# Attention feeding a top-1 mixture of experts on one core: the start, the row stores and the key tails of the attention stage written in another order and form

## The chip, the core and the metric

The kernel runs on one core of a Trainium2 chip. Its engines run side by side, each with an instruction stream of its own: TensorE (PE, with PEld for weight loads), VectorE (DVE), ScalarE (ACT), GpSimd (POOL), and SyncE (SP), which here only issues DMAs. The metric is the device time of one execution in microseconds (us), the median of several runs. Lower is better.

## The reference

Attention with capped scores over q, k, v of shape (4, 12, 448, 64), then eight experts of which each row takes the best one:

```python
scores = np.matmul(q, k.transpose(0, 1, 3, 2)) / np.sqrt(64)
scores = cap * np.tanh(scores / cap)
attn = softmax(scores)                       # over the keys
x = (attn @ v).transpose(0, 2, 1, 3).reshape(1792, 768)
logits = x @ w_gate                          # 8 experts
prob = softmax(logits);  eom = sigmoid(x @ w_output_gate)
for e in range(8):
    mask = logits.argmax(1) == e
    h = relu(x[mask] @ w1[e])                # 768 -> 1024
    out[mask] = prob[mask, e] * eom[mask, e] * (h @ w2[e])
```

The sum over the keys doesn't depend on their order. Products are made in three terms from planes hi and lo of each operand (hi is the operand rounded to fp32r, lo the rest).

## The kernel before

Attention runs over 24 units u (NU = 24); a unit is one batch and two heads, j = 0 and 1, which fill 128 partitions (64 each). Batch 2 is units 12 to 17, batch 3 units 18 to 23. For each unit the loop at L969 does, in this order of the program: three score blocks of 128 keys for both heads and one block for the "tail", the last 64 keys of both heads side by side (`qk`, matmuls L386 and L391, tanh on ACT into the tile `pt`, L393); the DMAs that are due (`load_ahead`); the K and Q planes of units to come (`turn_next`, DVE: a 32x32 block transpose L288, casts to hi L278, subtracts to lo L284); `exp` over the whole `pt` (L396, ACT); probabilities times V of the unit before (`pv`, L404); the evacuation of that result; the partial sums of the exponentials (`presum`, L413, L414, L418). Between these stand named slots ("f", "g", "h", "q", "e"), in which the work of the batch before (gate logits, row transposes, routing) is hung by a table `at`.

What sets the order around the change:

- `pt` has two buffers. The tanh of unit u+2 writes the buffer of unit u, and so comes after `presum(u)` and `pv(u)`. POOL does `presum` for units 0 to 19, DVE for units 20 to 23.
- Score blocks, row transposes (`trow`, L586) and gate results share three PSUM buffers in turn (`scores`). PE can't start the next block before the reader of the third last has finished.
- A tail's K planes are block diagonal: head 0's 64 keys on partitions 0 to 63, head 1's on 64 to 127, zeros elsewhere. Five pairs of K planes (PB = 5) are zeroed once at the start (L190, L191, twenty memsets), and each unit's tails are cast and subtracted as two separate 64x64 pieces.
- K and Q of units 3 and up come as raw tiles, for two units at a time in four DMAs (`load_pair`, L124). The numbers in `TURN` (L59) say how many of the plane preparations are made before and after the exponential of each unit; where it has no entry, (2, 0).
- Rows of the attention output go from `xr` tiles (L591, DVE) to the DRAM table `xs` by two DMAs each (L598). There are three `xr` buffers in turn. The six rows tasks of batch 2 are `rws[0]` to `rws[5]` (units 19 to 21), so `rws[3]` writes the buffer that `rws[0]` filled and must come after its store. The stores are kept in a list and issued on SP by `store_rows`, at the end of each unit and where the table says so.
- `load_v` (L110, L142) loads V of two units in six DMAs on SP: main part of u, tails of both, main part of u+1. The tails overwrite those of the units four before, and so come after `pv` of the later of these.
- `early()` is a routine of small steps on DVE (`nx`) which works out the first experts' row tables (tile `meta`, L646 to L656). `fd` fetches those tables by DMA (L849), `lds` loads expert weights (L826).
- At the start, POOL clears the tables in DRAM from the tile `tabi` (L220, L223), before its first `presum`; DVE makes the scale of the tanh (`icap`, L173, L174) and the constant `epsc`.

After the last unit the experts run (php and py, L1084) up to the end.

Of the kernel before, what the change touches and what calls it, by code (L numbers as in the profile page):

```python
# [22 lines left out]
def tile_kernel(ctx: ExitStack, tc, q, k, v, cap, w_gate, w_ogate, w1, w2, out):  # L23
    nc = tc.nc
# [10 lines left out]
    NE = 5  # L35
# [14 lines left out]
    for i, kind in enumerate((2, 4)):  # L50
# [9 lines left out]
            14: (2, 1), 15: (2, 1), 16: (1, 0), 17: (1, 0), 19: (1, 0), 20: (1, 0), 21: (0, 0)}  # L60
# [47 lines left out]
    def load_natural(dst, src, n, m, engs):  # L108
        for j in range(2):
            engs[j].dma_start(out=dst[:, 0:n, j], in_=src[j, 0:n * m].rearrange("(c p) d -> p c d", c=n))  # L110

    def load_nat(u, engs):
        (k0, q0), k_, q_ = nat[u], heads(k, u), heads(q, u)
        load_natural(k0, k_, NK, 128, engs)
        engs[1].dma_start(out=k0[0:64, NK], in_=k_[:, SK:S].rearrange("j p d -> p j d"))
        load_natural(q0, q_, NCH, CP, engs)

    def load_pair(src, u, tiles, to):
        t = raw1[tiles[u // 2 % 3]][:, 0:2 * S].rearrange("p (h r a) -> p h r a", h=2, a=32)
        lo = u % 2  # L120
        for c in range(4):
            x = c % 2
            h = c // 2 * NP + u % NP
            nc.sync.dma_start(  # L124
                out=t[32 * c:32 * c + 32, lo:].rearrange("p h r a -> p (h r) a"),
                in_=src[u // NP, h:h + 2 - lo, :, 32 * x:32 * x + 32].rearrange("h (r b) a -> b (h r) a", b=32))
        for i in range(lo, 2):
            to[u + i - lo] = t[:, i]

    def load_k(u):  # L130
        load_pair(k, u, (0, 1, 4), ldk)
# [64 lines left out]
    nc.vector.memset(ohc, 0.0)  # L198
    for p in range(NP):
        nc.vector.memset(ohc[:, p, p:p + 1], 1.0)  # L200

    wg = rtp.tile([128, NP, 2, 16], F32, name="wg")
    nc.vector.memset(wg, 0.0)
# [13 lines left out]
    tabi = rtp.tile([128, NTAB // 128, 2], F32, name="tabi")  # L217

# [38 lines left out]
    for g in range(4):  # L257
        for z, x in enumerate((2 * NT + g // 2, 4 * NT + g, 6 * NT + g, 6 * NT + 4 + g)):
            nc.vector.memset(part[32 * g:32 * g + 32, z:z + 1], float(x))
# [26 lines left out]
    def turned(src, n):  # L286
        ps = tbank([128, n], "tk")
        nc.vector.transpose(out=ps, in_=src.rearrange("p r a -> p (r a)"))  # L288
        return ps
# [21 lines left out]
    def first_planes(pk, pq):  # L311
        k_, (main, *tails) = k_parts(0, pk)
        q_, (q0,) = q_parts(0, pq)
        copy(True, main[0], main[2])
        copy(True, q0[0], q0[2])
        for x, z, y in (main, q0):
            minus(z, y, x)
        for x, z, y in tails:
            copy(False, x, y)
            minus(z, y, x)  # L320
        return k_ + q_

    def t_k(u):
        pl[u] = planes_of(k_parts(u, turned(ldk.pop(u), S)))
# [131 lines left out]
    def end_of_batch(b):  # L456
# [512 lines left out]
    for u in range(NU):  # L969
        if u % 2:  # L970
            load_v(u + 1)
        for s in range(NK):
            qk(u, s)
        if u == 0:
            pl[1] = planes_of(k_parts(1, nat_k(1)))
        if u > 0:
            load_ahead()
        qk(u, NK)
        if u == 0:
            pl[1] += planes_of(q_parts(1, nat_q(1)))  # L980
            nc.vector.memset(tabi, 0.0)
            load_wg()
            clear_tabs()
        if u == 1:
            pl[2] = planes_of(k_parts(2, nat_k(2)))
            pl[2] += planes_of(q_parts(2, nat_q(2)))
# [7 lines left out]
        if u > NU - 4:  # L994
            presum(u - 1, 0)
            presum(u - 1, 1)
# [10 lines left out]
        if u < NU - 4:  # L1007
            presum(u, 0)
        slot(u, "e")
# [350 lines left out]
```

## Time and profile before

| what | value |
|---|---|
| median of 3 runs | 515.81 us (515.36 to 515.87) |
| the profiled execution, its own time | 514.19 us |
| its span in the trace | 512.6 us |
| PE busy | 488.6 us, 95% |
| DVE busy | 381.3 us, 74% |
| ACT busy | 371.7 us, 73% |
| POOL busy | 288.8 us, 56% |

The profiled execution is 1.6 us below the median of the runs, and its time is 1.6 us more than the span. PE is the busiest engine, but the share is a mean over stages. Attention takes about the first 200 us, the experts the rest. The windows, the timelines of single engines and the ends of their idle time tell which engine the others wait for in each stage.

### The profile page before, as it was taken

The page shows a single profiled execution, that of the slowest core. Times are in us where ns is not written, and L with a number is a line of the kernel's source. Part 1 is how long each engine was busy: PE and PEld are TensorE (multiplying, and loading weights), DVE is VectorE, ACT ScalarE, POOL GpSimd, SP SyncE. Part 2 cuts the span into 40 slices and gives each one's busy share as a digit, 9 for nine tenths or more (in the row PEclk, how much of TensorE's full clock was granted, in tenths as well). Part 3 has the DMA queues.
Part 4 walks back from the last instruction along what each step waited for, and adds up shares of the span by engine and source line. Part 5 has one row for each costly group of instructions (what it writes and reads, how often), then busy time and mean ns, then how long its engine had stood idle before and what let it go on. Part 6 is the DMA issues. An engine that isn't in the chain of part 4 may idle for free. (4 is left out here: it accounts for less than half of the span.)

```text
span 512.6 us, 10021 instructions
## 1 busy us (share of the span) xinstructions
PE 488.6 (95%) x3069; PEld 341.1 (67%) x3069; DVE 381.3 (74%) x746; ACT 371.7 (73%) x433; POOL 288.8 (56%) x310
## 2 busy tenths in 40 slices
PE   7899999999999988999999999999999999999994
PEld 6444455444545543678989979988788867686691
DVE  7669999798686897988999878867676857555550
ACT  5888988889887868556589878858676867665551
POOL 4999998888988614962268861317265035352001
PEclk9999999999999989999999999999999999999998
DMA  6879868484532548884099336259759689991001
GB/s 144 168 134 162 142 108 144 91 146 83 87 70 49 86 61 287 316 271 130 2 350 407 115 104 245 62 207 368 272 191 394 263 308 362 336 359 67 1 33 49
DMA packets 152380, 91.92 MB, mean 179 GB/s; under 512 B 135027, under 2 KB 135163, under 8 KB 152321
## 3 DMA queue, kind: packets, MB, share of 16 engines
q1 hardware_dynamic: 142336, 58.24, 43.6%
q0 software_dynamic: 8832, 32.74, 17.3%
q8 instruction: 26, 0.43, 0.4%
q10 hardware_dynamic: 1152, 0.25, 0.2%
q14 instruction: 34, 0.27, 0.2%
HBM read 123.68 MB, written 12.04 MB: 265 GB/s over the span
## 5 line engine op out<-in xcount | busy, mean ns | idle before, releaser
L1063 DVE TENSOR_TENSOR wr<-raw,wr 128x768 fp32r<-128x768 f32 (+1 forms) x167 | 172.8, 1073 | 64.4 <-ACT wr L1062 63.5
L1062 ACT ACTIVATE wr<-raw 128x768 fp32r<-128x768 f32 (+1 forms) x167 | 150.6, 936 | 28.1 <-PE py L1084 12.4
L393 ACT ACTIVATE pt<-s,icap 128x896 f32<-128x896 f32 x96 | 80.1, 914 | 17.1 <-PE s L386 9.9
L404 PE MATMUL u<-pt,vv 128*64 128x448 f32 x384 | 79.1, 555 | 1.5 <-ACT pt L393 1.1
L1084 PE MATMUL py<-wr,hh 128*128 128x384 f32 x352 | 77.3, 340 | 0.0
L1084 PE MATMUL php<-wr,xh 128*128 128x512 f32 x264 | 74.8, 404 | 0.0
L1153 POOL DMA_INDIRECT out_dram<-yo,ti x13 | 21.7, 1668 | 90.8 <-ACT yo L1151 67.4
L396 ACT ACTIVATE pt<-pt,capc 128x3136 f32<-128x3136 f32 x24 | 69.9, 2912 | 0.6
L1084 PEld LDWEIGHTS py<-wr,hh 128*128 128x128 f32 x352 | 61.2, 188 | 4.0 <-issue 3.7
L1084 PEld LDWEIGHTS php<-wr,xh 128*128 128x128 f32 x264 | 47.4, 188 | 12.8 <-issue 2.5
L418 POOL TENSOR_TENSOR pb<-pb,pt 64x448 f32<-64x448 f32 x42 | 49.6, 1181 | 10.1 <-DVE pb L414 7.0
L404 PEld LDWEIGHTS u<-pt,vv 128*64 128x64 f32 x384 | 25.9, 139 | 42.6 <-issue 34.7
L413 POOL TENSOR_TENSOR pa<-pt 128x896 f32<-128x896 f32 x20 | 42.3, 2114 | 10.8 <-ACT pt L396 10.0
L1084 PE MATMUL py<-wr,hl 128*128 128x384 f32 x176 | 44.8, 335 | 0.0
L414 POOL TENSOR_TENSOR pb<-pa,pt 128x896 f32<-128x896 f32 x20 | 42.1, 2103 | 1.6
L1084 PE MATMUL php<-wr,xl 128*128 128x512 f32 x132 | 41.6, 396 | 0.9 <-DVE xl L878 0.9
L1084 PEld LDWEIGHTS py<-wr,hl 128*128 128x128 f32 x176 | 31.8, 188 | 0.0
L1200 POOL DMA_DIRECT2D rh<-in_moe_w_dram x42 | 23.2, 557 | 15.0 <-DVE wr L1063 8.9
L1084 PEld LDWEIGHTS php<-wr,xl 128*128 128x128 f32 x132 | 24.7, 187 | 7.3 <-DVE xl L878 1.3
L288 DVE STREAM_TRANSPOSE tk<-raw 128x448 f32<-128x448 f32 x42 | 27.5, 654 | 0.9
L1254 POOL DMA_INDIRECT out_dram<-yh,toh x6 | 6.1, 1011 | 35.5 <-issue 13.9
L591 DVE TENSOR_TENSOR xr<-trow,rec 112x512 f32<-112x512 f32 x24 | 16.1, 687 | 10.7 <-PE trow L586 9.7
(315 smaller groups left out, 812.2 us busy)
## 6 DMA issues: line engine op xcount, KB each, us to landing
raw<-in_moe_w_dram SPq DMA_DIRECT2D x78, 512.0 KB
raw<-in_moe_w_dram SPq DMA_DIRECT2D x104, 384.0 KB
rh<-in_moe_w_dram POOLq DMA_DIRECT2D x18, 512.0 KB, 7.2
rh<-in_moe_w_dram POOLq DMA_DIRECT2D x24, 384.0 KB, 8.6
raw<-in_q_dram SPq DMA_DIRECT2D x45, 112.0 KB
vv<-in_v_dram SPq DMA_DIRECT2D x48, 96.0 KB
raw<-in_k_dram SPq DMA_DIRECT2D x40, 112.0 KB
xs<-xr SPq DMA_DIRECT2D x36, 112.0 KB
```

What stands on the lines that cost most here:

```text
L288: nc.vector.transpose(out=ps, in_=src.rearrange("p r a -> p (r a)"))
L393: nc.scalar.activation(out=pt[u][:, 2 * s:2 * s + n], in_=ps, func=ACTF.Tanh, scale=icap)
L396: nc.scalar.activation(out=pt[u], in_=pt[u], func=ACTF.Exp, scale=capc)
L404: nc.tensor.matmul(ups[u][64 * j:64 * j + 64], lhsT=V[:, c, j, :], rhs=P[:, 2 * c + (j if c < NK else 0)], start=(c == 0), stop=(c == NK))
L413: eng.tensor_tensor(out=a, in0=P[:, 0:2], in1=P[:, 2:4], op=ALU.add)
L414: eng.tensor_tensor(out=s1[u], in0=a, in1=P[:, 4:6], op=ALU.add)
L418: eng.tensor_tensor(out=s1[u][h, j], in0=s1[u][h, j], in1=P[h, 2 * NK], op=ALU.add)
L1062: nc.scalar.activation(out=t[:, 0, 0:F], in_=raw, func=ACTF.Copy)
L1063: nc.vector.tensor_tensor(out=t[:, 1, 0:F], in0=raw, in1=t[:, 0, 0:F].bitcast(F32), op=ALU.subtract)
L1084: nc.tensor.matmul(ps[g][:, 0:n], lhsT=st[:, c], rhs=w[:, z, g * n:(g + 1) * n], start=(c == 0 and st is hi and z == 0), stop=(c == (KD, K ...
L1153: nc.gpsimd.indirect_dma_start(out=out, out_offset=bass.IndirectOffsetOnAxis(ap=ti, axis=0), in_=y, in_offset=None, bounds_check=NT - 1, o ...
L1200: nc.gpsimd.dma_start(out=d, in_=rows_of(src, e, w, c), **kw)
```

## The change

The diff has five parts.

1. Zeros and key order. The raw K tiles now hold 16 blocks of 32 columns for each unit: blocks 0 and 1 are head 0's first 64 keys (zeros for head 1), blocks 14 and 15 are head 1's last 64 keys (zeros for head 0). Head 0's tail is so its first 64 keys (T0 = 64) and head 1's its last 64; the V loads follow the same order. The zeros of the raw tiles are set once (six memsets). From unit 3 on a K preparation is two transposes (384 and 128 columns), one cast and one subtract of 128x512, with no separate tails. Only three pairs of K planes are still zeroed.
2. K loads. A pair of K tiles now comes in eight DMAs of half the size; Q is loaded as before.
3. Start. On DVE `icap` is made between the two first subtracts; `epsc`, the tails, `ohc` and `part` come later, and for units 1 and 2 the main part, Q and then the tails are made. POOL zeroes `wg` and `tabi` itself, ahead of all that it loads.
4. End of attention, SP: the last V load (units 22, 23) moves from the start of unit 21 into slot "q" of unit 20, ahead of `rws[1]` to `rws[3]` and of `store_rows`.
5. End of attention, DVE: `presum` of units 20 to 22 stands at the end of its own unit, not after the exponential of the next; the `nx` steps move behind the stores of unit 21; `TURN` prepares units 22 and 23 earlier or in other places.

```diff
-            14: (2, 1), 15: (2, 1), 16: (1, 0), 17: (1, 0), 19: (1, 0), 20: (1, 0), 21: (0, 0)}
+            14: (2, 1), 15: (2, 1), 16: (1, 0), 17: (1, 0), 20: (1, 0), 21: (0, 1), 22: (0, 0)}
...
+    def load_k(u):
+        t = kview[u // 2 % 3]
+        for i in range(u % 2, 2):
+            for c in range(4):
+                j, x = divmod(c, 2)
+                nc.sync.dma_start(
+                    out=t[32 * c:32 * c + 32, i, 2 * j:2 * j + 14],
+                    in_=blocks(k[u // NP, j * NP + u % NP + i - u % 2], x).rearrange("(r b) a -> b r a", b=32))
+            ldk[u + i - u % 2] = t[:, i]
...
-    for hl in kpl:
+    for hl in kpl[0:NN]:
...
+    for t in kview:
+        nc.vector.memset(t[0:64, :, 14:16], 0.0)
+        nc.vector.memset(t[64:128, :, 0:2], 0.0)
...
-    nc.vector.memset(wg, 0.0)
+    nc.gpsimd.memset(wg, 0.0)
...
+    nc.gpsimd.memset(tabi, 0.0)
...
+            nc.vector.transpose(out=ps[:, 0:SK], in_=src[:, 2:14].rearrange("p r a -> p (r a)"))
+            nc.vector.transpose(out=ps[:, SK:].rearrange("p (n k) -> p n k", n=2),
+                                in_=src.rearrange("p (n r) a -> p n (r a)", r=2)[:, 0::7])
...
+        if u >= NN:
+            return [hi, lo], [(hi, lo, ps)]
...
+            minus(main[1], main[2], main[0])
+            scales()
+        minus(q0[1], q0[2], q0[0])
...
-                  (1, "g"): [rws[0], rank_mm, place], (1, "h"): [place2, enter, scatter], (1, "q"): [rws[1], rws[2], rws[3], store_rows],
-                  (1, "e"): [nx] * 5,
-                  (2, "g"): [rws[4], rws[5]], (2, "h"): [nx, P(set_known, NE), store_rows],
-                  (2, "q"): [fd[0], fd[1], *lds[:2]],
+                  (1, "g"): [rws[0], rank_mm, place], (1, "h"): [place2, enter, scatter], (1, "q"): [P(load_v, NU - 2), rws[1], rws[2], rws[3], store_rows],
+                  (2, "g"): [rws[4], rws[5]], (2, "h"): [store_rows, *[nx] * 6, P(set_known, NE)],
+                  (2, "q"): [fd[0], *lds[:2], fd[1]],
...
-        if u % 2:
+        if u % 2 and u < NU - 3:
             load_v(u + 1)
...
-        if u > NU - 4:
-            presum(u - 1, 0)
-            presum(u - 1, 1)
...
-        if u < NU - 4:
+        if u < NU - 1:
             presum(u, 0)
+        if NU - 4 <= u < NU - 1:
+            presum(u, 1)
```

PE's and ACT's instructions keep their order; what moves is on DVE, POOL and SP. On DVE at the start, before (`tk` is unit 0's K turned by PE; the 64x64 rows are its tails):

```order
L284 TENSOR_TENSOR K0L<-tk_293,K0H 128x384
L284 TENSOR_TENSOR QL<-tq_298,QH 128x448
L278 CAST K0H<-tk_293 64x64
L284 TENSOR_TENSOR K0L<-tk_293,K0H 64x64
L278 CAST K0H<-tk_293 64x64
L284 TENSOR_TENSOR K0L<-tk_293,K0H 64x64
L173 RECIPROCAL icap<-capc 128x1
L174 TENSOR_SCALAR icap<-icap 128x1
L178 TENSOR_SCALAR epsc<-capc 128x1
L179 TENSOR_TENSOR epsc<-epsc,capc 128x1
```

and now:

```order
L302 TENSOR_TENSOR K0L<-tk_269,K0H 128x384
L186 RECIPROCAL icap<-capc 128x1
L187 TENSOR_SCALAR icap<-icap 128x1
L302 TENSOR_TENSOR QL<-tq_274,QH 128x448
L296 CAST K0H<-tk_269 64x64
L302 TENSOR_TENSOR K0L<-tk_269,K0H 64x64
L296 CAST K0H<-tk_269 64x64
L302 TENSOR_TENSOR K0L<-tk_269,K0H 64x64
L190 TENSOR_SCALAR epsc<-capc 128x1
L191 TENSOR_TENSOR epsc<-epsc,capc 128x1
```

The two rows that make `icap` stand ahead of the subtract to QL; all four tail rows and `epsc` come behind it.

On SP at the end of attention (`vv` is V, `xs<-xr` are the row stores; the first two of the ten are those of an earlier rows task, the next two those of `rws[0]`), before:

```order
L142 DMA vv_120<-in_v_dram 64x2x64 x2
L110 DMA vv_120<-in_v_dram 128x3x64 x2
L598 DMA xs<-xr 112x4x64 x10
L110 DMA vv_121<-in_v_dram 128x3x64 x2
L142 DMA vv_121<-in_v_dram 64x2x64 x2
L110 DMA vv_121<-in_v_dram 128x3x64 x2
L598 DMA xs<-xr 112x4x64 x4
```

and now:

```order
L155 DMA vv_120<-in_v_dram 64x2x64 x2
L113 DMA vv_120<-in_v_dram 128x3x64 x2
L626 DMA xs<-xr 112x4x64 x2
L113 DMA vv_121<-in_v_dram 128x3x64 x2
L155 DMA vv_121<-in_v_dram 64x2x64 x2
L113 DMA vv_121<-in_v_dram 128x3x64 x2
L626 DMA xs<-xr 112x4x64 x12
```

Eight of the ten stores, those of `rws[0]` to `rws[3]`, stand behind the six V loads.

On DVE in units 20 and 21 (`pa`, `pb` are the partial sums of unit 20, the first `xr` x3 are `rws[1]` to `rws[3]`, the x2 `rws[4]` and `rws[5]`; `bcnt` begins the `nx` steps), before, first the rows ahead of the `nx` steps and then, 24 rows later, those behind them:

```order
L567 TENSOR_SCALAR den<-den 112x4
L656 SCALAR_TENSOR_TENSOR den<-den 112x4
L569 RECIPROCAL ent<-den 112x4
L591 TENSOR_TENSOR xr<-trow,rec 112x512 x3
L649 TENSOR_TENSOR bcnt<-pre_245,ereg 1x8
```

```order
L649 TENSOR_TENSOR bo_2259<-bo_2259,boh 1x40
L646 TENSOR_REDUCE meta<-bo_2259 1x5
L591 TENSOR_TENSOR xr<-trow,rec 112x512 x2
L413 TENSOR_TENSOR pa<-pt 128x896
L414 TENSOR_TENSOR pb<-pa,pt 128x896
L418 TENSOR_TENSOR pb<-pb,pt 64x448 x2
```

and now:

```order
L683 SCALAR_TENSOR_TENSOR den<-den 112x4
L597 RECIPROCAL ent<-den 112x4
L619 TENSOR_TENSOR xr<-trow,rec 112x512 x3
L441 TENSOR_TENSOR pa<-pt 128x896
L442 TENSOR_TENSOR pb<-pa,pt 128x896
L446 TENSOR_TENSOR pb<-pb,pt 64x448 x2
L619 TENSOR_TENSOR xr<-trow,rec 112x512 x2
L676 TENSOR_TENSOR bcnt<-pre_237,ereg 1x8
```

The partial sums of unit 20 follow `rws[3]` at once, and the `nx` steps stand behind `rws[5]`.

## Rows read from the trace of the kernel before

**Rows 1.** windows: busy time of each engine (instructions), granted PE clock, DMA share, GB/s
```profile
60.00:120.00 60.00, 57.21 (x365) 28.12 (x363) 51.04 (x123) 51.54 (x50) 50.85 (x32) 1.00 0.65 117
...
186.00:188.00 2.00, 2.00 (x8) 0.50 (x6) 1.90 (x5) 1.97 (x3) 0.00 (x0) 0.50 0.13 14
...
300.00:400.00 100.00, 100.00 (x732) 84.75 (x731) 70.87 (x78) 71.81 (x97) 42.95 (x65) 1.00 0.66 242
```

**Rows 2.** timeline, ScalarE: start, duration, line, operation, count, idle before and its releaser
```profile
8.75 3.33 ACT L393 ACTIVATE pt<-s,icap 128x896 f32<-128x896 f32 x4 [2.16 <-DVE epsc L178]
12.12 2.92 ACT L396 ACTIVATE pt<-pt,capc 128x3136 f32<-128x3136 f32 x1
...
23.15 3.33 ACT L393 ACTIVATE pt<-s,icap 128x896 f32<-128x896 f32 x4 [1.96 <-PE s L386]
29.96 3.33 ACT L393 ACTIVATE pt<-s,icap 128x896 f32<-128x896 f32 x4 [0.54 <-POOL pb L418]
```

**Rows 3.** timeline, VectorE, start of the kernel
```profile
6.30 0.56 DVE L284 TENSOR_TENSOR K0L<-tk,K0H 128x384 fp32r<-128x384 f32 x1
...
8.30 0.16 DVE L173 RECIPROCAL icap<-capc 128x1 f32<-128x1 f32 x1
```

**Rows 4.** timeline, GpSimd, start of the kernel
```profile
13.63 0.60 POOL L220 DMA_DIRECT2D xs<-tabi  x1 [4.50 <-DVE tabi L981]
...
16.38 2.11 POOL L413 TENSOR_TENSOR pa<-pt 128x896 f32<-128x896 f32 x1
...
20.76 2.35 POOL L418 TENSOR_TENSOR pb<-pb,pt 64x448 f32<-64x448 f32 x2
```

**Rows 5.** timeline, VectorE, casts of one K and one Q preparation
```profile
184.82 0.94 DVE L278 CAST K3H<-tk 128x384 fp32r<-128x384 f32 x3
...
187.46 0.62 DVE L278 CAST QH<-tk 128x448 fp32r<-128x448 f32 x1
```

**Rows 6.** timeline, SyncE queue, V tails, V main and one pair of K
```profile
45.83 1.31 SPq L142 DMA_DIRECT2D vv<-in_v_dram  x2
47.19 1.12 SPq L110 DMA_DIRECT2D vv<-in_v_dram  x2
...
50.69 2.71 SPq L124 DMA_DIRECT2D raw<-in_k_dram  x4
```

**Rows 7.** timeline, ScalarE, units 22 and 23
```profile
183.72 3.33 ACT L393 ACTIVATE pt<-s,icap 128x896 f32<-128x896 f32 x4 [2.93 <-DVE pb L418]
...
192.34 3.33 ACT L393 ACTIVATE pt<-s,icap 128x896 f32<-128x896 f32 x4 [1.16 <-DVE pb L418]
```

**Rows 8.** timeline, TensorE, pv of 19, 21, 22, scores of 22, first expert
```profile
167.93 3.23 PE L404 MATMUL u<-pt,vv 128*64 128x448 f32 x16 [0.33 <-ACT pt L393]
...
181.50 0.38 PE L386 MATMUL s<-QL,K2H 64*128 64x448 f32 x2
...
185.68 4.90 PE L404 MATMUL u<-pt,vv 128*64 128x448 f32 x16
...
194.30 3.23 PE L404 MATMUL u<-pt,vv 128*64 128x448 f32 x16
...
205.59 0.74 PE L1084 MATMUL php<-wr,xl 128*128 128x512 f32 x2 [0.89 <-DVE xl L878]
```

**Rows 9.** timeline, VectorE, units 20 and 21
```profile
171.77 1.89 DVE L591 TENSOR_TENSOR xr<-trow,rec 112x512 f32<-112x512 f32 x3 [0.64 <-PE trow L586]
...
178.93 1.29 DVE L591 TENSOR_TENSOR xr<-trow,rec 112x512 f32<-112x512 f32 x2 [0.96 <-DMA xs<-xr]
180.13 1.08 DVE L413 TENSOR_TENSOR pa<-pt 128x896 f32<-128x896 f32 x1
```

**Rows 10.** timeline, SyncE queue, row stores
```profile
167.91 5.41 SPq L598 DMA_DIRECT2D xs<-xr  x4
```

**Rows 11.** windows around the row stores, columns as in Rows 1
```profile
168.50:170.50 2.00, 2.00 (x14) 0.72 (x10) 1.93 (x6) 2.00 (x1) 1.92 (x2) 1.00 0.58 115
170.50:172.40 1.90, 1.90 (x16) 1.28 (x12) 1.19 (x5) 0.93 (x2) 1.55 (x3) 1.00 0.00 0
```

More of the change, by code (lines that the diff above doesn't have):

```diff
@@ L106, in tile_kernel, with load_natural @@
     heads = lambda src, u: src[u // NP].rearrange("(j p) s d -> p j s d", j=2)[u % NP]
-    def load_natural(dst, src, n, m, engs):
+    T0 = S - SK
+    def load_natural(dst, src, n, m, engs, lo=0):
         for j in range(2):
-            engs[j].dma_start(out=dst[:, 0:n, j], in_=src[j, 0:n * m].rearrange("(c p) d -> p c d", c=n))
+            o = lo if j == 0 else 0
+            engs[j].dma_start(out=dst[:, 0:n, j], in_=src[j, o:o + n * m].rearrange("(c p) d -> p c d", c=n))
     def load_nat(u, engs):
@@ new lines, in tile_kernel @@
+    kview = [raw1[i].rearrange("p (h r a) -> p h r a", h=2, a=32) for i in KT]
+    blocks = lambda src, x: src[..., 32 * x:32 * x + 32]
+    def load_k(u):
[7 more added lines that the diff above has]
+            ldk[u + i - u % 2] = t[:, i]
@@ L120, in load_pair, with load_q @@
+    def load_q(u):
+        t = raw1[QT[u // 2 % 3]][:, 0:2 * S].rearrange("p (h r a) -> p h r a", h=2, a=32)
         lo = u % 2
         for c in range(4):
-            x = c % 2
-            h = c // 2 * NP + u % NP
+            j, x = divmod(c, 2)
+            h = j * NP + u % NP
             nc.sync.dma_start(
                 out=t[32 * c:32 * c + 32, lo:].rearrange("p h r a -> p (h r) a"),
-                in_=src[u // NP, h:h + 2 - lo, :, 32 * x:32 * x + 32].rearrange("h (r b) a -> b (h r) a", b=32))
+                in_=blocks(q[u // NP, h:h + 2 - lo], x).rearrange("h (r b) a -> b (h r) a", b=32))
@@ L256, in tile_kernel, with late_consts @@
     part = const.tile([128, 4], F32, name="part")
-    for g in range(4):
-        for z, x in enumerate((2 * NT + g // 2, 4 * NT + g, 6 * NT + g, 6 * NT + 4 + g)):
-            nc.vector.memset(part[32 * g:32 * g + 32, z:z + 1], float(x))
+    def late_consts():
+        nc.vector.memset(ohc, 0.0)
+        for p in range(NP):
+            nc.vector.memset(ohc[:, p, p:p + 1], 1.0)
+        for g in range(4):
+            for z, x in enumerate((2 * NT + g // 2, 4 * NT + g, 6 * NT + g, 6 * NT + 4 + g)):
+                nc.vector.memset(part[32 * g:32 * g + 32, z:z + 1], float(x))
     ereg = const.tile([1, E], F32, name="ereg")
@@ L287, in turned @@
         ps = tbank([128, n], "tk")
-        nc.vector.transpose(out=ps, in_=src.rearrange("p r a -> p (r a)"))
+        if n == S:
+            nc.vector.transpose(out=ps, in_=src.rearrange("p r a -> p (r a)"))
+        else:
+            nc.vector.transpose(out=ps[:, 0:SK], in_=src[:, 2:14].rearrange("p r a -> p (r a)"))
+            nc.vector.transpose(out=ps[:, SK:].rearrange("p (n k) -> p n k", n=2),
+                                in_=src.rearrange("p (n r) a -> p n (r a)", r=2)[:, 0::7])
         return ps
@@ L309, in planes_of, with first_planes @@
         return ts
[L311 to L317, printed above, removed]
+    def first_planes(u, mid=lambda: None):
+        ts, (main, *tails) = k_parts(u, nat_k(u))
+        if u:
+            copy(False, main[0], main[2])
+            minus(main[1], main[2], main[0])
+        mid()
+        q_, (q0,) = q_parts(u, nat_q(u))
+        if u:
+            copy(False, q0[0], q0[2])
+        else:
+            copy(True, main[0], main[2])
+            copy(True, q0[0], q0[2])
+            minus(main[1], main[2], main[0])
+            scales()
+        minus(q0[1], q0[2], q0[0])
         for x, z, y in tails:
@@ L973, in tile_kernel @@
             qk(u, s)
-        if u == 0:
-            pl[1] = planes_of(k_parts(1, nat_k(1)))
         if u > 0:
             load_ahead()
-        qk(u, NK)
         if u == 0:
-            pl[1] += planes_of(q_parts(1, nat_q(1)))
-            nc.vector.memset(tabi, 0.0)
+            first_planes(1, lambda: qk(0, NK))
+        else:
+            qk(u, NK)
+        if u == 0:
+            late_consts()
             load_wg()
```

39 lines of the change are left out of this document (15 added, 24 removed).

## Prediction

> **What bounds the kernel now.** I read the windows first. Between 60 and 120 us PE is busy 57.21 of 60 us and DVE 51.04; from 300 to 400 us, in the experts, PE is busy the whole 100 us [rows 1]. So in the middle of attention and in the experts only less PE work or a faster clock could help, and the change leaves PE's instructions and their order alone. What it can move is the time at which the steady stage begins and the time at which the experts begin. The timelines of those two places are the next views.
>
> At the start ACT's first tanh waits 2.16 us, last for DVE's scale operations [rows 2]: DVE makes QL, then four small tail operations, and only at 8.30 begins the scale [rows 3]. The third tanh (unit 2) waits 1.96 us. The profile names PE there, but GpSimd's first partial sum, whose `pt` buffer that tanh overwrites, ends at 20.76 + 2.35 = 23.11, right ahead of the tanh at 23.15; I read GpSimd as the true releaser, and the fourth tanh names it [rows 2, 4]. GpSimd began that sum at 16.38, though exp of unit 0 ended at 12.12 + 2.92 = 15.04; it was still issuing the clearing DMAs, for which it had waited 4.50 us on DVE's `tabi` [rows 2, 4].
>
> At the end ACT waits 2.93 us for DVE's partial sum of unit 20 ahead of tanh 22, and 1.16 us ahead of tanh 23 [rows 7]. DVE begins that sum only at 180.13, behind the `nx` steps and a wait of 0.96 us for a row store [rows 9]. The gap costs PE its clock as well: granted 0.50 from 186 to 188 us, the lower of its two levels (1.2 GHz) [rows 1], and pv of unit 21 takes 4.90 us against 3.23 for the others [rows 8]. Last, the first expert's second product waits 0.89 us for DVE [rows 8].
>
> **Start: 1.9 us gained.** From the start of the scale at 8.30 to the tanh are 0.45 us, in which three small operations stand; the two that make the scale take about 0.3. K0L's subtract at 6.30 takes 0.56 [rows 3], so with the pair behind it QL's subtract begins near 7.1; it is a little longer than K0L's (448 columns, 0.6) and ends at 7.7. One pair of score matmuls on it (0.4: two of the sixteen that pv does in 3.23 [rows 8]) leads to a tanh at about 8.1 in place of 8.75: some 0.7 gained [rows 2]. The tails now come while PE does the three full blocks, which hide them. exp of unit 0 then ends at 14.34. GpSimd's clearing took 13.63 to 16.38, 2.75 us; without the wait for DVE it can start at 13.63 - 4.50 = 9.13, with 0.5 us for the new memsets at 9.6, and is done by 12.4, ahead of exp [rows 4]. The first partial sum so starts at 14.34, 2.04 earlier, and ends at 21.07. tanh 2 then starts about 21.2 and tanh 3, bound by GpSimd too, about 28.0 where it was 29.96 [rows 2]. From there on PE is the bound and all is shifted by 1.9. Bounds: 2.1 at best; 0 if PE's block really was what tanh 2 waited for.
>
> **Middle: nothing.** A K preparation's three casts take 0.94 us; one of 448 columns takes 0.62, so 512 columns about 0.70 [rows 5]. Cast and subtract save 0.24 each, and the second transpose gives back some 0.15. That is about 0.33 us in each of 21 units, 7 us of DVE, on an engine that isn't the bound there: 0 on the path, at best 1 us where waits are short. Eight K DMAs in place of four, at 2.71 / 4 = 0.68 us each of SP time, add at most 2.7 us of SP time per pair [rows 6]. The loads are made units ahead of use; if that slack were gone, the price would be those 2.7 us at one place.
>
> **End, what is taken away.** The partial sum of unit 20 now stands right behind the third `xr`, and the `nx` steps come later. With nothing new in its way tanh 22 would wait only for its first score block, whose last pair ends at 181.88 [rows 8], and start at 181.95; a unit without waits takes about 7 us (tanh 2 to tanh 3: 6.81 [rows 2]; I take 7.2), so tanh 23 at 189.15, 3.2 us before 192.34 [rows 7]. The experts' wait of 0.89 also goes, since the sum of unit 22 no longer stands ahead of it. Together -4.1.
>
> **End, what is added.** On SP the six V loads of units 22 and 23 now stand ahead of the stores of `rws[0]`. Their tails overwrite those of unit 19 and wait for its pv, which ends at 167.93 + 3.23 = 171.16 [rows 8]; behind the tails come two main loads. Tails and main took 45.83 to 48.4 elsewhere, 2.57 us [rows 6]. So the stores of `rws[0]`, which went out from 167.91 [rows 10], go out at about 173.7 and 174.15. The third `xr` of the row at 171.77 (`rws[3]`) writes the buffer that they read. Before, they had long landed and it ended at 173.66 [rows 9]; now DVE stands still there, behind it the partial sum of unit 20, and PE, which needs the PSUM buffer that this `xr` reads for the third score block of unit 21. Let L be the landing of the second store; the third `xr` ends at T = L + 0.8.
>
> How T sets the end: from the end of the third `xr` to tanh 22 there are 181.95 - 173.66 = 8.3 us of work; PE has done a little of it while it waits, and may lose clock over the gap as it did for pv of 21 (+1.7). I take T + 8.6 for tanh 22 (T + 7.7 to T + 9.6) and T + 15.8 for tanh 23. Against 192.34, with the start (-1.9) and the experts' wait (-0.9), the whole change is T + 15.8 - 192.3 - 2.8 = T - 179.3 = L - 178.5.
>
> How late is L? Bounded by two rows of the same kind of store. The pair issued from 167.91 moved in a window of 115 GB/s that ended at 170.50, with no DMA traffic after it [rows 11]: about 2.2 us behind the second issue, which gives L = 176.4 and -2.1. The next pair, issued behind the `xr` at 171.77 + 0.7, is what DVE still waited for until 178.93 [rows 9, 10], some 6.0 us; that gives L = 180.2 and +1.7. I take 177.1: nearer the first, because these stores now lead the burst instead of following it, and 0.7 later, because 256 KB of V stand just ahead of them, some 2.2 us at 115 GB/s, partly over by then. So L - 178.5 = **-1.4**, 515.8 - 1.4 = 514.4 us.
>
> The Trainium skill, "DMA: Bandwidth & Descriptors", section "Anatomy of one DMA — SWDGE (gpsimd) path", puts one DMA at about 2.0 us plus its bytes over 436 GB/s, an estimate of 2.3 us for 112 KB; it would give L = 176.4 and a gain of 2. The row that ended at 178.93 speaks against it as a general price here.
>
> **Rivals.** (A) Slower: the stores land late. The mechanism is the one above with L = 180.2: the V loads and GpSimd's row-table scatters are in flight when the stores go out. It decides from L = 178.5 on, every us later costs one. For it: the 6 us case of the same stage. Against it: that case stood in a queue of eight stores. Time 515.8 + 1.7 = 517.5. In the Trainium skill, same page, section "Queues, rings and completion order", a DMA counts as done only after every earlier write of the same DMA engine, across its queues; by that the scatters would hold these stores back and A is what follows. The row that ended at 178.93 agrees; the pair issued at 167.91 doesn't need it.
>
> (B) Nothing waits in the new place: the stores land before DVE comes to `rws[3]`. That is the -4.1 of the end with -1.9 of the start, 509.8 us. It would need stores landed by 173.0, before they can be issued by my count, so it takes V loads that don't wait.
>
> (C) The start's gain isn't there, because PE's block and not GpSimd released tanh 2, or because doubled K loads land late: -1.4 + 1.9 = +0.5, 516.3 us.
>
> (D) The landing lies between the two rows, L = 178.4: 515.8, no change. This is also where the edit does what it says on DVE and the wait for the store takes all of it back.
>
> **How the numbers follow.** Forecast with L near 177: 0.42, its own range 512.8 to 515.2. A 0.25, B 0.06, C 0.13, D 0.14. A measurement here can tell about 0.2%, 1.03 us, from no change. Faster by more: most of the forecast (0.38), B (0.06) and a little of D (0.02), 0.46. Within: the forecast's rest (0.04), most of C (0.10), D (0.10), a little of A (0.03), 0.27. Slower: A (0.22), C (0.03), D (0.02), 0.27. The likeliest is 514.4. The range leaves out B below and the last tenth of A above: from 512.3 (start 2.1 and L = 176.4 with the smallest of the T spans) to 518.0 (A with 0.5 of lost clock).
>
> **What would show it.** In the profile of the changed kernel, in its own clock: tanh 0 near 8.05, GpSimd's first sum near 14.3, tanh 3 near 28.0. After that every unit of the middle 1.9 us earlier with PE's share unchanged; DVE with 7 us less work. At the end DVE's third `xr` of `rws[1]` to `rws[3]` with a wait for `xs<-xr`, of 2 to 4 us, and PE idle ahead of the third score block of unit 21; no wait of ACT for `pb` ahead of tanh 22 beyond that. If that DVE wait ends near 178 or later in the shifted clock, A holds. If there is none, B does. I am wrong altogether if the time is set by something that I put at nothing: K loads that come late in the middle, V loads that hold up pv of 22, or `meta` steps that now end too late for the first expert's gather.

## The result

The changed kernel takes 518.81 us (median of 8 runs, 517.41 to 520.62) against 515.84 (515.36 to 516.33): a ratio of 1.0056, 95% interval 1.004 to 1.0072. It is slower, by 3.0 us, where 1.4 us less were forecast, and lies just above the range. Its profiled execution took 517.53 us with a span of 515.8, 3.2 us more than the span before.

The start went nearly as forecast. ScalarE and GpSimd of the changed kernel (start, duration, line, operation, idle before and its releaser), to set against [rows 2] and [rows 4]:

```profile
8.45 3.35 ACT L421 ACTIVATE pt<-s,icap 128x896 f32<-128x896 f32 x4 [1.23 <-PE s L414]
...
21.71 3.33 ACT L421 ACTIVATE pt<-s,icap 128x896 f32<-128x896 f32 x4 [0.81 <-PE s L414]
...
28.40 3.33 ACT L421 ACTIVATE pt<-s,icap 128x896 f32<-128x896 f32 x4 [0.42 <-POOL pb L446]
```

```profile
8.29 2.15 POOL L236 DMA_DIRECT2D tab<-tabi  x4
14.83 2.09 POOL L441 TENSOR_TENSOR pa<-pt 128x896 f32<-128x896 f32 x1 [4.39 <-ACT pt L424]
```

GpSimd's clearing is over long before exp of unit 0, the first sum begins at 14.83 for 16.38, and tanh 3 at 28.40 for 29.96: 1.56 us gained.

The loss is at one place. VectorE, TensorE and the SyncE queue in units 20 and 21, to set against [rows 8] to [rows 10]:

```profile
171.01 1.29 DVE L619 TENSOR_TENSOR xr<-trow,rec 112x512 f32<-112x512 f32 x2 [1.34 <-PE trow L614]
180.06 0.69 DVE L619 TENSOR_TENSOR xr<-trow,rec 112x512 f32<-112x512 f32 x1 [7.76 <-DMA xs<-xr]
180.67 1.08 DVE L441 TENSOR_TENSOR pa<-pt 128x896 f32<-128x896 f32 x1
...
184.51 1.29 DVE L619 TENSOR_TENSOR xr<-trow,rec 112x512 f32<-112x512 f32 x2 [0.34 <-PE trow L614]
```

```profile
167.17 3.23 PE L432 MATMUL u<-pt,vv 128*64 128x448 f32 x16 [0.33 <-ACT pt L421]
...
172.91 0.37 PE L414 MATMUL s<-QL,K1H 64*128 64x448 f32 x2
180.81 0.74 PE L414 MATMUL s<-QH,K1H 64*128 64x448 f32 x2 [7.54 <-DVE xr L619]
...
184.83 3.23 PE L432 MATMUL u<-pt,vv 128*64 128x448 f32 x16
```

```profile
170.42 1.30 SPq L155 DMA_DIRECT2D vv<-in_v_dram  x2
171.77 1.12 SPq L113 DMA_DIRECT2D vv<-in_v_dram  x2
```

```profile
172.99 0.96 SPq L626 DMA_DIRECT2D xs<-xr  x2
```

The V tails go out when pv of unit 19 has ended (170.40), the two stores of `rws[0]` at 172.99 and about 173.5, and DVE's third `xr` waits 7.76 us for them, until 180.06. Behind it stands the sum of unit 20, and PE waits 7.54 us for the PSUM buffer that this `xr` reads. PE's granted clock is down over the gap and after it (columns as in [rows 1]):

```profile
176.50:180.50 4.00, 0.00 (x0) 0.00 (x0) 0.44 (x1) 0.00 (x0) 0.00 (x0) 0.61 0.64 110
180.50:182.00 1.50, 1.19 (x6) 0.83 (x6) 1.47 (x3) 0.00 (x0) 0.00 (x0) 0.50 0.22 41
182.00:184.00 2.00, 2.00 (x8) 1.53 (x7) 1.95 (x3) 1.26 (x2) 0.00 (x0) 0.50 0.42 84
```

What follows runs without the old waits. ScalarE's third tanh of unit 21 (the row at 182.34) and its tanh of units 22 and 23, against [rows 7], and the first expert, against the last of [rows 8]:

```profile
182.34 1.01 ACT L421 ACTIVATE pt<-s,icap 128x896 f32<-128x896 f32 x1 [7.67 <-PE s L414]
...
189.80 3.33 ACT L421 ACTIVATE pt<-s,icap 128x896 f32<-128x896 f32 x4 [1.12 <-PE s L414]
...
196.40 3.32 ACT L421 ACTIVATE pt<-s,icap 128x896 f32<-128x896 f32 x4
```

```profile
207.56 1.19 PE L1110 MATMUL php<-wr,xh 128*128 128x512 f32 x4
208.59 0.63 PE L1110 MATMUL php<-wr,xl 128*128 128x512 f32 x2
```

tanh 23 starts 4.06 us later than before, the first php at 207.56 for 203.51. The wait of 0.89 us for `xl` in the first expert is gone, and the span ends 3.2 us later.

### The profile page after: what moved, and what is told of

It is laid out like the page before. It is cut to its first block, busy times and chain, and to the rows that moved or that the text cites. A ratio compares the mean times of both kernels' runs of the same rounds, so it can differ in the third digit from the quotient of the medians.

```text
span 515.8 us, 10013 instructions
## 1 busy us (share of the span) xinstructions
PE 488.1 (95%) x3069; PEld 342.9 (66%) x3069; DVE 376.7 (73%) x679; ACT 371.6 (72%) x433; POOL 289.3 (56%) x312
## 5 line engine op out<-in xcount | busy, mean ns | idle before, releaser
L432 PE MATMUL u<-pt,vv 128*64 128x448 f32 x384 | 77.5, 545 | 1.5 <-ACT pt L421 1.1
L605 POOL DMA_INDIRECT tab<-ent,posi x16 | 16.0, 1000 | 13.4 <-DVE ent L597 8.9
## 6 DMA issues: line engine op xcount, KB each, us to landing
raw<-in_moe_w_dram SPq DMA_DIRECT2D x78, 512.0 KB
rh<-in_moe_w_dram POOLq DMA_DIRECT2D x18, 512.0 KB
```

The source lines that it names most:

```text
L432: nc.tensor.matmul(ups[u][64 * j:64 * j + 64], lhsT=V[:, c, j, :], rhs=P[:, 2 * c + (j if c < NK else 0)], start=(c == 0), stop=(c == NK))
```

## The experiments

The theory after the result: the row stores, put behind the V loads, land so late that the `xr` buffer isn't free; all else of the change gains. What was open was why they landed 6.6 us behind the second issue (173.47 to 180.06), when 2.95 had been taken. Each kernel below was timed beside the kernel before on the same chip, whose medians there were 516.0 to 516.7.

### Undoing the order on SP

`e1_store_first`: only the two stores of `rws[0]` go ahead of the V loads.

```diff
-(1, "q"): [P(load_v, NU - 2), rws[1], rws[2], rws[3], store_rows],
+(1, "q"): [store_rows, P(load_v, NU - 2), rws[1], rws[2], rws[3], store_rows],
```

> The changed kernel with one call moved: in slot q of unit 20 the two stores of rws[0] are issued ahead of the six V loads, not behind them. In the changed kernel the third xr (rws[3]) waits 7.76 us for those stores, until 180.06. Theory (the wait for the store, put behind the V loads, sets the end): the stores go out near 167.2 and land by 170, DVE has no wait for xs<-xr at its third xr, PE none of 7.5 us, and the time is 6 to 8 us below the changed kernel's, about 511. Rival (V loads or DVE order of the end are at fault, the store wait only covers another one): a new wait of about the same size appears at the same place and the time stays within 2 us of the changed kernel's.

515.31 us, ratio 0.9973 (0.9954 to 0.9993). The third `xr` no longer waits; but the fourth, which writes the buffer of `rws[1]`, now does, since that store still stands behind the V loads. VectorE:

```profile
170.52 1.89 DVE L619 TENSOR_TENSOR xr<-trow,rec 112x512 f32<-112x512 f32 x3 [1.30 <-PE trow L614]
...
180.50 0.69 DVE L619 TENSOR_TENSOR xr<-trow,rec 112x512 f32<-112x512 f32 x1 [4.67 <-DMA xs<-xr]
```

The place of the stores decides, as the theory says, but the gain was less than expected, because the same wait comes back two rows later: tanh 22 and 23 wait instead.

`e4_loadv_back` and `h2_loadv_back2` (the same kernel twice): the whole V load back at the start of unit 21.

```diff
-(1, "q"): [P(load_v, NU - 2), rws[1], rws[2], rws[3], store_rows],
+(1, "q"): [rws[1], rws[2], rws[3], store_rows],
...
-        if u % 2 and u < NU - 3:
+        if u % 2:
             load_v(u + 1)
```

> The changed kernel with its V loads of units 22 and 23 put back to the start of unit 21, as in the kernel before; all else as changed. The stores of rws[0] then stand alone at the end of unit 20's queue again, right behind the earlier store. Theory: they land before the third xr needs them, no DVE wait for xs<-xr at 172; the V loads come later, as before; the time is 5 to 8 us below the changed kernel's, 511 to 513. Rival: the later V loads stand behind ten stores and hold up pv of unit 22, or the fourth and fifth xr wait for the stores of rws[1] until about 178; then within 3 us of the changed kernel's.

> The changed kernel with its V loads back at the start of unit 21, once more and in more rounds: 511 to 512, ratio to before 0.989 to 0.994.

511.46 us, 0.9916 (0.9882 to 0.995), and again 512.04 us, 0.9898 (0.9875 to 0.9922). This beats both kernels. VectorE and ScalarE of the second:

```profile
170.87 1.89 DVE L619 TENSOR_TENSOR xr<-trow,rec 112x512 f32<-112x512 f32 x3 [1.40 <-PE trow L614]
172.67 1.08 DVE L441 TENSOR_TENSOR pa<-pt 128x896 f32<-128x896 f32 x1
...
176.98 0.69 DVE L619 TENSOR_TENSOR xr<-trow,rec 112x512 f32<-112x512 f32 x1 [0.80 <-DMA xs<-xr]
178.52 0.69 DVE L619 TENSOR_TENSOR xr<-trow,rec 112x512 f32<-112x512 f32 x1 [0.85 <-DMA xs<-xr]
```

```profile
181.03 3.33 ACT L421 ACTIVATE pt<-s,icap 128x896 f32<-128x896 f32 x4 [1.13 <-PE s L414]
...
189.46 3.33 ACT L421 ACTIVATE pt<-s,icap 128x896 f32<-128x896 f32 x4 [1.71 <-DVE pb L446]
```

The three `xr` run without a break, the sum of unit 20 follows at 172.67, and tanh 22 starts at 181.03 for 183.72 before. To be faster than before, the kernel needs nothing else of the change undone.

`h1_v_first_alone`: the kernel before with the V loads put ahead, and nothing else of the change. Its diff is the one of `e4_loadv_back` the other way round.

> The kernel before with the V loads of units 22 and 23 put ahead of rws[1] to rws[3] and of store_rows alone (part 4); DVE's order, the start and the keys as before. Theory: the third xr waits 6 to 8 us for the stores of rws[0], until about 181.5, PE stands still as long ahead of the third score block of unit 21, and the kernel is 4 to 8 us slower than before. Rival (only together with the new DVE order does it hurt): within 2 us of the kernel before.

521.17 us, 1.0083 (1.0055 to 1.0112). VectorE, the third `xr`:

```profile
181.72 0.69 DVE L591 TENSOR_TENSOR xr<-trow,rec 112x512 f32<-112x512 f32 x1 [8.00 <-DMA xs<-xr]
```

The wait is 8.00 us without the new DVE order too. Moving the V loads alone costs some 4.5 us.

### Why the store lands late

`e3_two_stores`: the stores of `rws[1]` and `rws[2]` are listed behind that of `rws[3]`, so that for the time of the wait only two stores are in flight.

```diff
+    def alone():
+        stores.insert(1, stores.pop())
...
-(1, "q"): [P(load_v, NU - 2), rws[1], rws[2], rws[3], store_rows],
+(1, "q"): [P(load_v, NU - 2), rws[1], rws[2], rws[3], alone, store_rows],
```

> The changed kernel, but the stores of rws[1] and rws[2] are listed behind that of rws[3] and so can't be issued before the third xr is done; behind the V loads only the two stores of rws[0] are in flight. Rival Q (six stores share the DMA engines): the wait of the third xr falls from 7.76 us to 4 or 5, ending near 177, and the time falls by 2 to 3 us. Theory S (the scatters hold the landing back): the wait stays at 7 to 8 us.

518.64 us, 1.0043 (1.0028 to 1.0058). VectorE, and windows of one us (the last two columns are the DMA engines' busy share and GB/s):

```profile
180.44 0.69 DVE L622 TENSOR_TENSOR xr<-trow,rec 112x512 f32<-112x512 f32 x1 [8.03 <-DMA xs<-xr]
```

```profile
173.00:174.00 1.00, 0.40 (x4) 0.01 (x1) 0.00 (x0) 1.00 (x2) 0.70 (x2) 1.00 0.36 84
174.00:175.00 1.00, 0.00 (x0) 0.00 (x0) 0.00 (x0) 0.78 (x1) 0.70 (x2) 1.00 0.62 78
175.00:176.00 1.00, 0.00 (x0) 0.00 (x0) 0.00 (x0) 0.00 (x0) 0.58 (x1) 1.00 0.77 161
176.00:177.00 1.00, 0.00 (x0) 0.00 (x0) 0.00 (x0) 0.00 (x0) 0.00 (x0) 0.57 0.25 51
177.00:178.00 1.00, 0.00 (x0) 0.00 (x0) 0.00 (x0) 0.00 (x0) 0.00 (x0) 0.50 0.24 52
178.00:179.00 1.00, 0.00 (x0) 0.00 (x0) 0.00 (x0) 0.00 (x0) 0.00 (x0) 0.50 0.03 5
179.00:180.00 1.00, 0.00 (x0) 0.00 (x0) 0.00 (x0) 0.00 (x0) 0.00 (x0) 0.50 0.00 0
```

The wait is 8.03 us, no shorter, while from 176 on the DMA engines are a quarter busy and from 178 nearly idle. So it is not a matter of bandwidth shared with the stores behind: that rival fell.

`e2_scatter_late`: the last routing step and GpSimd's four scatters come behind the third `xr`.

```diff
-(1, "h"): [place2, enter, scatter], (1, "q"): [P(load_v, NU - 2), rws[1], rws[2], rws[3], store_rows],
+(1, "h"): [place2], (1, "q"): [P(load_v, NU - 2), rws[1], rws[2], rws[3], store_rows],
-(2, "g"): [rws[4], rws[5]],
+(2, "g"): [enter, scatter, rws[4], rws[5]],
```

> The changed kernel, but the last routing step (enter) and GpSimd's four row-table scatters come only after the third xr of unit 20 (in slot g of unit 21). The stores and the V loads stay as they are. Theory S (the scatters in flight hold back the landing of the stores): the third xr ends its wait about 3 us sooner, near 177, and the stores land 2.5 to 3.5 us after the second issue instead of 6.6; the time falls by up to 3 us unless the later tables hold up the first experts. Rival Q (the six stores issued one after the other share the DMA engines, so that the first lands with the last): no change in that wait, 7 to 8 us.

515.55 us, 0.998 (0.9965 to 0.9995), 3 us less than the changed kernel. `k1_only_scatters_late` leaves the routing step where it was and holds back the scatters alone, by splitting the reduction to `posi` off from `place2`:

```diff
-            nc.vector.tensor_reduce(out=posi, in_=rk, axis=AX.X, op=ALU.max)
+            if b != B - 2:
+                place3()
...
+        def place3():
+            nc.vector.tensor_reduce(out=posi, in_=rt["rk"], axis=AX.X, op=ALU.max)
...
-(1, "h"): [place2, enter, scatter], (1, "q"): [P(load_v, NU - 2), rws[1], rws[2], rws[3], store_rows],
+(1, "h"): [place2, enter], (1, "q"): [P(load_v, NU - 2), rws[1], rws[2], rws[3], store_rows],
-(2, "g"): [rws[4], rws[5]],
+(2, "g"): [place3, scatter, rws[4], rws[5]],
```

> The changed kernel; the last routing step on DVE stays where it is, and only GpSimd's four scatters come behind the third xr, held by the row positions (posi), one reduction that is moved behind the sum of unit 20. Scatters hold the landing: the third xr waits 3.5 to 4.5 us, as with step and scatters moved (3.81). Rival (the DVE step's place makes the difference, not the scatters): 7 to 8 us, as in the changed kernel (7.76).

`k2_quiet` is that kernel with the list of `e3_two_stores` besides, so that only the V loads and two stores are in flight.

> As the kernel with only the scatters late, and the stores of rws[1] and rws[2] besides listed behind that of rws[3], so that only the V loads and the two stores of rws[0] are in flight. If the store's quiet price (about 2.2 us behind its second issue, from the pair at 167.91 in the kernel before) holds: the third xr waits about 3 us, until some 2.5 to 3 us behind the second issue. If the V loads hold it: the wait stays at 3.8 us or more.

The third `xr` on VectorE, of `e2_scatter_late`, `k1_only_scatters_late` and `k2_quiet`:

```profile
175.77 0.69 DVE L619 TENSOR_TENSOR xr<-trow,rec 112x512 f32<-112x512 f32 x1 [3.81 <-DMA xs<-xr]
```

```profile
175.04 0.69 DVE L623 TENSOR_TENSOR xr<-trow,rec 112x512 f32<-112x512 f32 x1 [3.76 <-DMA xs<-xr]
```

```profile
174.78 0.69 DVE L626 TENSOR_TENSOR xr<-trow,rec 112x512 f32<-112x512 f32 x1 [3.63 <-DMA xs<-xr]
```

| kernel | scatters in flight | stores in flight | first store issued | third `xr` goes on | wait, us |
|---|---|---|---|---|---|
| changed | 4 | 6 | 172.99 | 180.06 | 7.76 |
| `e3_two_stores` | 4 | 2 | 173.09 | 180.44 | 8.03 |
| `g2_half_late` | 2 | 6 | 172.51 | 178.78 | 6.96 |
| `e2_scatter_late` | 0 | 6 | 172.65 | 175.77 | 3.81 |
| `k1_only_scatters_late` | 0 | 6 | 171.97 | 175.04 | 3.76 |
| `k2_quiet` | 0 | 2 | 171.83 | 174.78 | 3.63 |

Each wait in the table is that of one profiled execution. With the scatters away the store lands about 3.0 us behind its first issue, whether six or two stores are in flight; with the four scatters it takes 7.1 to 7.4. That the DVE step's place is the cause is ruled out by `k1_only_scatters_late`. In `k2_quiet` the wait of 3.63 us lies between what was expected (3, or 3.8 and more); the landing, 2.5 us behind the second issue, is at the quiet price.

GpSimd's first and last scatter in the changed kernel, and the first that follows the pair at 167.91 in the kernel before:

```profile
170.74 0.96 POOL L605 DMA_INDIRECT tab<-ent,posi  x1 [0.28 <-POOL pb L446]
...
174.52 0.96 POOL L605 DMA_INDIRECT tab<-ent,posi  x1 [0.30 <-issue]
```

```profile
172.21 0.96 POOL L577 DMA_INDIRECT tab<-ent,posi  x1 [0.28 <-POOL pb L418]
```

The delay has two parts. The same V loads and two stores are moved in `k2_quiet` by these windows:

```profile
172.00:173.00 1.00, 0.12 (x2) 0.00 (x0) 0.00 (x0) 1.00 (x2) 0.00 (x0) 1.00 0.83 185
173.00:174.00 1.00, 0.00 (x0) 0.00 (x0) 0.00 (x0) 0.51 (x1) 0.00 (x0) 1.00 1.00 208
174.00:175.00 1.00, 0.00 (x0) 0.00 (x0) 0.23 (x1) 0.00 (x0) 0.00 (x0) 1.00 0.10 22
```

There the data go at about 200 GB/s and are through shortly after 174, 2.5 us behind the first store's issue; DVE goes on at 174.78. In `e3_two_stores`, with the scatters, they go at 84, 78, 161, 51 and 52 GB/s and are through shortly after 178, 5.1 us behind the issue; DVE goes on only at 180.44. So with the scatters on their way the data themselves come some 2.6 us later, and the signal that the store is done comes another 1.8 us later. What in the scatters does either stays open.

`g2_half_late` keeps two scatters early and holds two back, by making `ent` in two halves.

```diff
+            if b == B - 2:
+                nc.vector.reciprocal(out=ent[:, b, 0:2, 1], in_=den[:, 0, 0:2])
+                return
...
+        def enter2():
+            nc.vector.reciprocal(out=ent[:, b, 2:4, 1], in_=rt["den"][:, 0, 2:4])
+            scatter((2, 3))
...
-(1, "h"): [place2, enter, scatter],
+(1, "h"): [place2, enter, P(scatter, (0, 1))],
-(2, "g"): [rws[4], rws[5]],
+(2, "g"): [enter2, rws[4], rws[5]],
```

> The changed kernel with two of the four scatters where they are and two behind the third xr. Theory S: the third xr's wait for the stores ends between that with no scatter (3.81 us) and with four (7.76 us), at 5 to 6.5 us, and the time lies between 515.5 and 518.8. Rival (it is not the scatters but that DVE's last routing step is done later): with that step's first half in its old place the wait is back at 7 to 8 us.

516.89 us, 1.0006 (0.9986 to 1.0026); the wait is 6.96 us, above the 5 to 6.5 that were expected and close to the rival's 7 to 8, so that only `k1_only_scatters_late` rules this rival out. Two scatters hold the store nearly as long as four: the delay doesn't grow in step with their number. The time itself lies in the middle. GpSimd had issued both by 172.44, just before the store went out.

Taking the scatters away doesn't repair the kernel: `k1_only_scatters_late` took 517.14 us, 1.002 (0.9956 to 1.0085), and `k2_quiet` 516.69, 0.9989 (0.995 to 1.0028), though their experts begin at 202.6 to 202.7, sooner than before. The row tables now come late, and GpSimd waits for the gather that hangs on them ahead of its part of the last partial sum (4.8 us in both). PE comes to that sum only behind the first expert's first products; it then waits 3.5 and 3.0 us for it, and its granted clock is 0.83 on the mean from 210 to 220 us. There the early begin is lost. `g1_both` does it with the V loads put back as well:

```diff
-(1, "h"): [place2, enter, scatter], (1, "q"): [rws[1], rws[2], rws[3], store_rows],
+(1, "h"): [place2], (1, "q"): [rws[1], rws[2], rws[3], store_rows],
-(2, "g"): [rws[4], rws[5]],
+(2, "g"): [rws[4], rws[5], enter, scatter],
...
-        if u % 2 and u < NU - 3:
+        if u % 2:
```

> The changed kernel with its V loads back at the start of unit 21 and the last routing step and the scatters behind the fifth xr of unit 21, so that neither V loads nor scatters are in flight with the row stores. Theory S (scatters hold the stores' landing): no wait of DVE for xs<-xr at the fourth and fifth xr (0.73 and 1.33 us with the V loads put back alone), tanh 22 and 23 up to 1 us sooner; whether the time falls below the 511.46 of that kernel hangs on the row tables, which now come about 5 us later: 509 to 513. Rival (the V loads hold the landing): those waits stay.

513.03 us, 0.9923 (0.9896 to 0.9949), no better than without it. The fourth and fifth `xr` no longer wait for the stores, as the theory wants (VectorE):

```profile
175.84 1.29 DVE L619 TENSOR_TENSOR xr<-trow,rec 112x512 f32<-112x512 f32 x2
```

But GpSimd and then PE wait for the tables. GpSimd's and PE's waits from 190 and 200 us on (line, what for, us in total, times, longest), in an execution of 517.68 us; how much of them the median of 513.03 pays isn't shown:

```profile
POOL pb L446 <- DMA xg<-xs,ti: 6.1, 1, 6.1
```

```profile
PE sm L465 <- POOL pb L446: 4.3, 1, 4.3
```

`h3_nx_last` is the kernel with the V loads put back, as in `e4_loadv_back`, and with the `nx` steps, the first table fetches and weight loads moved behind the sum of unit 21:

```diff
-(2, "h"): [store_rows, *[nx] * 6, P(set_known, NE)],
-(2, "q"): [fd[0], *lds[:2], fd[1]],
+(2, "h"): [store_rows],
+(2, "e"): [*[nx] * 6, P(set_known, NE), fd[0], *lds[:2], fd[1]],
```

> The kernel with the V loads put back, and besides the nx steps, the first table fetches and the first weight loads moved behind the sum of unit 21 (slot e of unit 21, not h and q). Theory (tanh 23 waits 2.16 us because that sum stands behind the nx steps): the wait goes, tanh 23 2 us sooner, 509.5 to 510.5. Rival (the row tables are then late for the first experts, as they came about 3 us later): a wait of PE or DVE for xg or raw ahead of the first php, no gain or a loss of up to 3 us.

521.85 us, 1.0084 (1.0059 to 1.0108): the rival held, and worse than it said. In its profiled execution (524.61 us) PE waited 4.8 us for the last sum and 3.0 for the gather.

### The other parts alone

`f3_start_only` is the kernel before with part 3, `f2_keys_only` with parts 1 and 2, `f1_start_and_keys` with parts 1 to 3; the hunks are those of the change.

> The kernel before with the start alone as changed (part 3); key tails, K loads and the end as before. Theory: GpSimd's first sum at about 14.4, tanh 3 near 28.0 to 28.4 for 29.96, and 1.5 to 2.2 us gained in all; no 0.5 to 0.6 us wait between the first and second tanh of unit 20, which showed with the changed keys alone too. Rival (the start's gain is given back at the end, where DVE is late with the sum of unit 20): under 0.8 us gained.

> The kernel before with the raw keys' zeros, the key order and the eight K loads alone (parts 1 and 2); start and end as before. Theory: 7 us less work on DVE, nothing on the path: within 0.2% of the kernel before. Rival (DVE waits in the late units or the K loads matter): faster or slower by over 1 us.

> The kernel before with the start and the key tails as changed (parts 1 to 3), and the end of attention (parts 4 and 5) as before. Theory (the start's gain of 1.5 to 2 us lasts to the experts): tanh 3 at 28.0 to 28.4, unit 20's tanh 1.5 to 2 us earlier than before, experts 1.5 to 2 us earlier, ratio 0.996 to 0.997. Rival (about half is lost where unit 20 waited 0.6 us more in the changed kernel): the same 0.5 to 0.6 us wait of ACT between the first and second tanh of unit 20, and 0.8 to 1.3 us gained.

| kernel | median, us | ratio to before | interval |
|---|---|---|---|
| `f3_start_only` | 515.08 | 0.9963 | 0.9948 to 0.9977 |
| `f2_keys_only` | 515.76 | 0.998 | 0.9959 to 1.0 |
| `f1_start_and_keys` | 513.53 | 0.9934 | 0.9909 to 0.9959 |
| `h2_loadv_back2`: parts 1 to 3 and 5 | 512.04 | 0.9898 | 0.9875 to 0.9922 |
| changed kernel: all parts | 518.81 | 1.0056 | 1.004 to 1.0072 |

The start gains 1.9 us (0.37% of 516), the keys about 1, at the edge of what can be told from nothing. Together they gain 3.4, more than the 0.996 to 0.997 expected of `f1_start_and_keys`. The new order on DVE at the end adds another 1.9 by `h2_loadv_back2` (0.9934 to 0.9898) and 0.9 by the same kernel's other measurement, `e4_loadv_back` (0.9916); the intervals overlap, so that it adds anything isn't shown. The V loads alone turn a gain of some 5 us into a loss of 3.

ACT's wait of 0.4 to 0.6 us between the first and second tanh of unit 20 (0.63 in the changed kernel's profile, none before) isn't the keys' doing, as I had thought: it shows in `f3_start_only` and `h1_v_first_alone` too, and not in `k1_only_scatters_late`. Its cause stays open.

## Why the prediction was wrong

**What bounds the kernel, and the start**: right. tanh 0 came 0.30 us sooner where 0.7 was forecast: the hi cast of K0 itself began at 5.75, later than its 5.40 before. The main term, GpSimd's sum, carried: 1.56 us at tanh 3 in the profile, 1.9 us by the ratio of `f3_start_only`. GpSimd, not PE, had held tanh 2: in `h1_v_first_alone`, whose start is that of before, the profile names GpSimd's `pb` for the same wait (1.97 us).

**The middle**: right in kind. A K preparation's rows on VectorE:

```profile
163.39 0.58 DVE L309 STREAM_TRANSPOSE tk<-raw 128x384 f32<-128x384 f32 x1
164.00 0.33 DVE L310 STREAM_TRANSPOSE tk<-raw 128x128 f32<-128x128 f32 x1
164.37 0.69 DVE L296 CAST K3H<-tk 128x512 fp32r<-128x512 f32 x1
165.09 0.69 DVE L302 TENSOR_TENSOR K3L<-tk,K3H 128x512 fp32r<-128x512 f32 x1
```

Cast and subtract take 0.69 each, as estimated (0.70); the two transposes 0.58 and 0.33 against one of 0.62 to 0.66. So the second transpose gives back some 0.26 us for each K preparation, where 0.15 was taken. DVE's busy time fell by 4.6 us (381.3 to 376.7), not 7, and the keys alone moved the time by at most 2 us, 1 by the median. The doubled K loads cost nothing that shows.

**End, what is taken away**: right for tanh 22, not for tanh 23. With the stores in their old place (`h2_loadv_back2`) tanh 22 starts at 181.03; the forecast of 181.95 less the 1.7 us that tanh 3 gained there (28.25) is 180.2, so some 0.8 us of waits remain. tanh 23 starts at 189.46 there, where 189.15 less 1.7 is 187.4: it still waits 1.71 us for the sum of unit 21, for which the forecast had nothing. Of the 3.2 us forecast at tanh 23, 1.2 come out there; in the changed kernel, where the store's wait delays everything else, this doesn't show. The wait of 0.89 us went in every kernel with the new DVE order, but also in `f3_start_only` and `h1_v_first_alone`, which keep the old one, so the order isn't shown to be the reason.

**End, what is added**: the chain was right, one term was not. The V tails went out at pv's end, the stores 2.57 us behind them, as worked out. From the third `xr`'s end to tanh 23 I had 15.8 us: 196.40 - (180.06 + 0.69) is 15.65. That is partly luck: tanh 22 came 9.05 us behind that end where 8.6 was taken, and tanh 23 6.6 behind tanh 22 where 7.2 was. The term that failed is L, the landing of the second store of `rws[0]`. I chose between two rows, 2.2 and 6.0 us behind the second issue, and took 2.95, nearer to the first, "because these stores now lead the burst instead of following it". It measured 6.6, above even the upper row. (The 2.3 us that the prediction had from the Trainium skill stands there for DMAs issued by GpSimd; these stores go out on SyncE.) `e3_two_stores` shows that leading the burst doesn't help, since the burst isn't what delays. What told the two rows of before apart was whether scatters were on their way: the pair from 167.91 went out with none, the next one among four, and the stores now go out among the same four. The prediction had named the scatters under rival A and then weighed the rows by the queue. Why 6.6 is above the upper row's 6.0 isn't shown; the V loads ahead may have a part in it, since in `h2_loadv_back2`, where they stand behind, the stores of `rws[1]` were done 5.0 us behind their second issue (171.94 to 176.98) among the same four scatters.

L is 3.6 us of the 4.6 by which the profiled span missed (3.2 more where 1.4 less was forecast; 4.4 by the medians). Another 1.1 is the start's gain, taken as 1.9: the profile shows 1.56 at tanh 3 and only 0.76 by pv of unit 19 (ended 170.40 for 171.16), part of it lost in the wait of unit 20 that stayed open.

The rivals: A is what happened, at 3.0 us where 1.7 was its price. B is close to what the kernel without the V move does (511.5 to 512.0; B's 509.8 has no wait at all, and there the fourth and fifth `xr` still wait 0.8 each and tanh 23 1.71). C and D fell.

The Trainium skill, "DMA: Bandwidth & Descriptors", section "Queues, rings and completion order", says that a DMA's completion is signalled only after every earlier write of the same DMA engine, across its queues. The runs agree in direction: with the scatters of another queue in flight the same store is done 7.1 us behind its first issue, without them 3.1, and in `e3_two_stores` the DMA engines were nearly idle over the last two us of it. No run shows which write the signal waited for. The rule covers only that last part: it doesn't say why the data were moved more slowly before, nor why two scatters hold the store nearly as long as four.

## What to carry to other kernels

A load that is moved earlier in a queue is charged with what it waits for itself: here V tails waited for pv, and stores behind them became late for a buffer that is used three rows later. Before moving a DMA, list what stands behind it in that queue, and which engine reuses the buffers that those transfers hold. When a landing time has to be taken from rows, take the row with the same other transfers in flight, not the one with the same place in the queue.

## What the runs showed of the hardware

- A store of 112 KB to DRAM, issued with its twin, was done about 2.5 us behind the second issue in `k2_quiet` (about 172.3 to 174.78) and 6.6 us with GpSimd's scatters of small entries in flight; in `e3_two_stores` the DMA engines moved 84 and 78 GB/s over two us of that time where they moved 185 and 208 in `k2_quiet`, and their busy share was 0.03 and 0.00 over two us, from 178 to 180, in which DVE was still waiting.
- After a gap of 7.54 us PE's granted clock was 0.50, the lower of its two levels, in the last microseconds of the gap and until 184 at least, over 3 us into the new work; the first pair of score matmuls behind it took 0.74 us, the last ahead of it 0.37, so the gap cost more than its own length.
